# GpSimd in program order, low parts of the second layer on VectorE, and a joint form of the later heads

## The chip, the core and the metric

The kernel runs on one core of a Trainium2 chip. The metric is the time of one execution on the device in microseconds (us). The core has five engines that run side by side, each with its own instruction queue: PE (TensorE, matrix products; its weight loads are shown apart as PEld), DVE (VectorE), ACT (ScalarE), POOL (GpSimd) and SP, which only issues DMAs. An engine works through its queue in order and stands still at an instruction whose inputs are not there. POOL also issues DMAs here.

## The reference

Windowed attention, then a two-layer network on its output:

```python
scores = q @ k.T / 8                       # 8 batches, 8 heads, 576 positions, 64 wide
# heads 0-3: key within 32 positions back; heads 4-7: every 4th key within 128 back
attn = exp(masked - max); attn = attn / (attn.sum(-1) + 1e-9)
x = (attn @ v) laid out as [4608 tokens, 512]
h = x @ w_in                               # [512, 2048], float64 input
g = where(h >= 1, h, where(h <= -1, 0, (h + 1) ** 2 / 4))
out = g @ w_out                            # [2048, 512]
```

## The kernel before

**Attention.** Two heads are handled together: "head n" below is such a pair, 0 to 31, four to a batch. Queries are cut into 18 blocks of 32, and each block meets 64 keys. `scores` makes 36 small matmuls into two PSUM banks and adds the mask (L151, one DVE instruction for each of the two heads of the pair, `j`). `softmax` runs L165 to L171: the row maximum on DVE, the subtraction on POOL, the exponential on ACT, the row sum, + EPS (L169) and the reciprocal on DVE, the multiplication on POOL. The weights are then transposed, on PE for heads 0 to 11 (`transpose_pe`, L196, copied out by ACT in L204) and on DVE for heads 12 to 31 (`transpose`, L185, twelve instructions of 32x192 for each head), and `values` (L236) multiplies by v: 36 matmuls, each 64 keys deep and 32 queries wide. One matmul in this precision shows as two records in the trace.

**Network.** Numbers are kept as a high part (rounded by ACT, L284) and a low part (a subtraction, L285, on DVE or POOL), and three products of parts make one product. `split` does both. Tokens 0 to 511 go through `layer1` and `layer2` directly while the weights are turned from float64 into parts (`weights`), summed (`combine`) and written to `stream` in DRAM. The other 4096 tokens go in four passes p = 1 to 4 of 1024 tokens, where each layer is a seven-product scheme (Strassen-Winograd) on halves: `macro1` makes 56 units in the first layer, `macro2` 56 in the second; each unit is six matmuls. In the second layer unit j is product kk = j // 8 of column block u = j % 8. `make_part(p, j + 4)` prepares the operand of a unit four units ahead: for kk = 1 and kk = 2 it first combines blocks of g on DVE (L521, L523, L527), then splits. The low part goes to DVE for odd u, to POOL for even u. `ops_x` prepares the seven operands x of the next pass, four of the low parts on POOL.

**Order.** PE and SP follow the program; the order of the instructions on DVE, ACT and POOL is chosen by a scheduler from estimated costs and priorities. For passes 1 to 4 `seq` lists the units, and `place(i, fn)` hangs other work before unit i of that list: head i of a pass has its scores and softmax at base + 9i + 3, its transposes at + 9, its values at + 15. Weights are read back from `stream` by DMAs on POOL (L609), nine units ahead, into five buffers that hold two units each. In the first stage (tokens 0 to 511) `slots` does the same for heads 4 to 11.

## Time and profile before

| | us |
|---|---|
| median of 3 runs | 1048.84 (1047.24 to 1049.14) |
| the profiled execution | 1050.84 |
| its span, first to last instruction | 1049.1 |
| PE busy in the span | 904.7 (86%) |
| DVE busy | 735.1 (70%) |
| POOL busy | 554.3 (53%) |
| ACT busy | 506.9 (48%) |

The span is one execution seen by the hardware profiler; 1.7 us lie around it. Shares of busy time are means over stages that differ, so the rows further down are taken by stage: 0 to 225 us is the first stage (heads 0 to 11, the first 512 tokens, the weights), then the four passes follow, each with a first layer and a second layer. PE has two speeds; the profile gives the granted clock as a share of the full one, and in a stretch at the low level each matmul takes about twice as long.

### The profile page before, as it was taken

The page shows a single profiled execution, that of the slowest core. Times are in us where ns is not written, and L with a number is a line of the kernel's source. Part 1 is how long each engine was busy: PE and PEld are TensorE (multiplying, and loading weights), DVE is VectorE, ACT ScalarE, POOL GpSimd, SP SyncE. Part 2 cuts the span into 40 slices and gives each one's busy share as a digit, 9 for nine tenths or more (in the row PEclk, how much of TensorE's full clock was granted, in tenths as well). Part 3 has the DMA queues.
Part 4 walks back from the last instruction along what each step waited for, and adds up shares of the span by engine and source line. Part 5 has one row for each costly group of instructions (what it writes and reads, how often), then busy time and mean ns, then how long its engine had stood idle before and what let it go on. Part 6 is the DMA issues. An engine that isn't in the chain of part 4 may idle for free.

```text
span 1049.1 us, 19802 instructions
## 1 busy us (share of the span) xinstructions
PE 904.7 (86%) x7990; PEld 729.5 (70%) x7990; DVE 735.1 (70%) x1039; ACT 506.9 (48%) x779; POOL 554.3 (53%) x466
## 2 busy tenths in 40 slices
PE   4668777989988886999988797999995999999898
PEld 3656565767776664887767575887784888887686
DVE  6877888568878997447778997367869932457743
ACT  2544555444444534435535435434465443656353
POOL 2545566574434668753335465733346674324674
PEclk7578987999899888999999788999898999999899
DMA  9579983787566553786666553785453677666565
GB/s 363 206 267 347 376 286 137 267 275 231 170 188 189 165 176 115 206 245 202 192 186 191 148 165 104 237 242 154 123 163 115 172 211 229 200 192 181 145 196 161
DMA packets 104922, 212.90 MB, mean 203 GB/s; under 512 B 7872, under 2 KB 20352, under 8 KB 102784
## 3 DMA queue, kind: packets, MB, share of 16 engines
q0 software_dynamic: 60928, 117.45, 39.1%
q1 hardware_dynamic: 43904, 94.20, 25.6%
q8 instruction: 63, 1.03, 0.4%
q14 instruction: 27, 0.22, 0.1%
HBM read 172.82 MB, written 38.80 MB: 202 GB/s over the span
## 4 chain that ended last, share of the span: by engine, by line
PE 41%; DVE 32%; ACT 8%; POOL 8%; issue 7%; DMA 2%; SPq 1%; POOLq 0%; DVEq 0%; ACTq 0%
PE o_b L541 12%; PE o_c L541 8%; DVE pt L185 7%; PE h_b L470 7%; DVE g L463 4%; PE h_c L470 3%; ACT pt L459 3%; PE o_a L541 3%; DVE pt L456 3%; PE o L236 2%; POOL c L171 2%; DVE g L505 2%; PE acc L382 2%; ACT pt L462 2%; DVE m L319 2%
## 5 line engine op out<-in xcount | busy, mean ns | idle before, releaser
L470 PE MATMUL h_b<-x,wi 128*128 128x512 f32 x768 | 201.4, 407 | 23.4 <-DVE pt L456 11.5
L470 PEld LDWEIGHTS h_b<-x,wi 128*128 128x128 f32 x768 | 147.4, 195 | 60.9 <-DVE pt L456 14.1
L609 POOL DMA_DIRECT2D wi<-stream_wi x112 | 81.8, 731 | 139.8 <-PE h_b L470 62.7
L541 PE MATMUL o_b<-parts,wo 128*128 128x512 f32 x384 | 104.1, 414 | 27.0 <-DVE parts L285 19.7
L463 DVE SCALAR_TENSOR_TENSOR g<-pt 128x1536 f32<-128x1536 f32 (+1 forms) x64 | 82.0, 1302 | 57.1 <-ACT pt L462 56.5
L284 ACT CAST part<-g 128x512 fp32r<-128x512 f32 x112 | 69.3, 621 | 89.3 <-PE o_c L541 37.3
L609 POOL DMA_DIRECT2D wo<-stream_wo x112 | 82.7, 739 | 55.2 <-PE o_b L541 23.4
L541 PEld LDWEIGHTS o_b<-parts,wo 128*128 128x128 f32 x384 | 74.2, 198 | 47.1 <-DVE parts L285 22.5
L285 POOL TENSOR_TENSOR part<-g,part 128x512 fp32r<-128x512 f32 x56 | 78.6, 1404 | 53.6 <-ACT part L284 49.3
L470 PE MATMUL h_c<-x,wi 128*128 128x512 f32 x384 | 104.0, 407 | 1.7 <-DVE out L395 1.7
L185 DVE STREAM_TRANSPOSE pt<-c 32x192 f32<-32x192 f32 x240 | 88.5, 369 | 21.7 <-POOL c L171 18.6
L236 PEld LDWEIGHTS o<-pt,v 64*64 64x64 f32 x2160 | 77.0, 151 | 34.9 <-issue 12.7
L236 PE MATMUL o<-pt,v 64*64 64x32 f32 x2160 | 81.5, 233 | 22.7 <-ACT pt L204 7.7
L284 ACT CAST parts<-g 128x512 fp32r<-128x512 f32 x112 | 69.0, 620 | 61.0 <-PE o_b L541 25.4
L285 POOL TENSOR_TENSOR parts<-g,parts 128x512 fp32r<-128x512 f32 x56 | 78.6, 1404 | 37.0 <-ACT parts L284 35.9
L541 PE MATMUL o_b<-part,wo 128*128 128x512 f32 x384 | 94.1, 390 | 1.6 <-DVE part L285 1.6
L459 ACT ACTIVATE pt<-pt,consts 128x1536 f32<-128x1536 f32 x32 | 50.5, 1579 | 85.9 <-DVE pt L456 85.9
L285 DVE TENSOR_TENSOR part<-g,part 128x512 fp32r<-128x512 f32 x56 | 48.9, 874 | 60.9 <-ACT part L284 60.9
L470 PEld LDWEIGHTS h_c<-x,wi 128*128 128x128 f32 x384 | 74.5, 195 | 19.7 <-ACT out L395 2.1
L166 POOL TENSOR_TENSOR c<-c 96x768 f32<-96x768 f32 x28 | 47.2, 1687 | 76.7 <-DVE c L165 76.7
L541 PEld LDWEIGHTS o_b<-part,wo 128*128 128x128 f32 x384 | 71.8, 188 | 17.6 <-DVE part L285 2.4
L171 POOL TENSOR_TENSOR c<-c 96x768 f32<-96x768 f32 x30 | 52.8, 1759 | 51.7 <-DVE c L170 43.2
(104 smaller groups left out, 1694.9 us busy)
## 6 DMA issues: line engine op xcount, KB each, us to landing
wi<-stream_wi POOLq DMA_DIRECT2D x112, 512.0 KB, 4.3
wo<-stream_wo POOLq DMA_DIRECT2D x112, 512.0 KB, 4.1
v<-v_in SPq DMA_DIRECT2D x30, 576.0 KB, 4.3
k<-k_in SPq DMA_DIRECT2D x30, 304.0 KB, 5.0
...
```

Source lines behind the costliest of these rows:

```text
L166: eng.tensor_tensor(out=c, in0=c, in1=spread(0), op=ALU.subtract)
L171: nc.gpsimd.tensor_tensor(out=c, in0=c, in1=spread(2), op=ALU.mult)
L185: nc.vector.transpose(out=pt[r : r + 32, :, g], in_=c[32 * g : 32 * g + 32, j, :, 32 * h : 32 * h + 32],)
L236: PE.matmul(out=ops[part][r, QB * i : QB * i + QB], lhsT=hd["v"][r, at], rhs=hd["pt"][r, QB * at : QB * at + QB], start=True, stop=True,)
L284: nc.scalar.copy(out=out_hi, in_=src)
L285: lo_engine.tensor_tensor(out=out_lo, in0=src, in1=out_hi.bitcast(F32), op=ALU.subtract)
L456: nc.vector.tensor_tensor(out=o, in0=a, in1=b, op=ALU.add)
L459: nc.scalar.activation(out=src, in_=src if first_in is None else first_in, func=AF.Prelu, bias=minus_t, alpha=0.5)
L463: nc.vector.scalar_tensor_tensor(out=dst, in0=src, scalar=1.0, in1=src, op0=ALU.min, op1=ALU.mult)
L470: PE.matmul(out=bk, lhsT=w[:, a, 128 * c : 128 * c + 128], rhs=X[p, kk][:, x, c], start=STARTS[kk] and c == 0 and n == 0, stop=STOPS[kk] a ...
L541: PE.matmul(out=bk, lhsT=w[:, a, 128 * m : 128 * m + 128], rhs=s[:, x], start=STARTS[kk] and u == 0 and n == 0, stop=STOPS[kk] and u == NU ...
L609: nc.gpsimd.dma_start(out=t, in_=stream[name][i0 : i0 + 2].rearrange("c p h x -> p c h x"))
```

## The change

1. POOL follows the program order too, like PE and SP. `softmax` is cut into `exps` and `normalise`, which are placed by hand: at + 5 and + 8 of a later head, and in the slots behind the scores in the first stage.
2. In the second layer the low part goes to DVE for three of four u (kk > 0), and for one of four u at kk = 0.
3. Heads 12 to 31: one mask instruction for both heads of the pair, six transposes of 32x384 instead of twelve of 32x192 into one zeroed buffer `pts`, and values in 12 matmuls over 128 keys and 96 queries; v is loaded in a layout of its own (`v2`). Heads are 11 units apart instead of 9. The + EPS goes from DVE to ACT for all heads.
4. `stream` is 28 small tensors for each layer, and a read of two units takes one row of 4 KB for each partition, where it took two of 2 KB.
5. The steps of `ops_x` move: two POOL splits 16 and 12 units ahead of the rest, the others behind the last head's values. In the first stage the stores of weights and their preparation are put in another order.

```diff
+    pts = const.tile([128, 2, NB // 3, 96], F32, name="pts")
...
+    stream = {
+        n: [dram.tile([128, 2, 2, 256], F32, name=f"stream_{n}{i}") for i in range(7 * NU // 2)]
+        for n in ("wi", "wo")
+    }
...
+    def banks_of(which, name):
+        if which is None:
+            both = ps.tile([128, 2, TOK], F32, tag="att", name=name)
+            return both, [both[:, 0], both[:, 1]]
+        return None, [bank(i, f"{name}_{i}") for i in which]
...
+        else:
+            vt = hd["v"][:, : NB // 3 * 2 * D]
+            nc.sync.dma_start(out=vt, in_=v2[n - EARLY])
+            hd["v"] = vt.rearrange("p (j t d) -> p j t d", j=2, d=D)
...
+            else:
                 nc.vector.tensor_tensor(
-                    out=c[:, j],
-                    in0=sps[j][:96, : 6 * KW].rearrange("p (t x) -> p t x", x=KW),
-                    in1=msk[:, kind],
+                    out=c.rearrange("p j t x -> p j (t x)"),
+                    in0=both[:96, :, : 6 * KW],
+                    in1=msk[:, kind].rearrange("p t x -> p (t x)").unsqueeze(1).broadcast_to([96, 2, 6 * KW]),
                     op=ALU.add,
                 )
...
+        engine.tensor_tensor(out=c, in0=c, in1=spread(n, 0), op=ALU.subtract)
...
+    def normalise(n, engine):
+        c, st = heads[n]["c"], heads[n]["st"]
         nc.vector.tensor_reduce(out=st[:, 1], in_=c, op=ALU.add, axis=AX.X)
-        nc.vector.tensor_scalar(out=st[:, 1], in0=st[:, 1], scalar1=EPS, scalar2=None, op0=ALU.add)
+        nc.scalar.activation(out=st[:, 1], in_=st[:, 1], func=AF.Copy, bias=EPS)
         nc.vector.reciprocal(out=st[:, 2], in_=st[:, 1])
-        nc.gpsimd.tensor_tensor(out=c, in0=c, in1=spread(2), op=ALU.mult)
...
     def transpose(n):
-        c, pt = heads[n]["c"], new_pt(n).rearrange("p (t g i) -> p t g i", g=3, i=QB)
-        for j in range(2):
-            for g in range(3):
-                for h in range(2):
-                    r = 64 * j + 32 * h
-                    nc.vector.transpose(
-                        out=pt[r : r + 32, :, g],
-                        in_=c[32 * g : 32 * g + 32, j, :, 32 * h : 32 * h + 32],
-                    )
-
-    def transpose_pe(n, banks):
-        c, pt = heads[n]["c"], new_pt(n)
-        for i, (t0, t1) in enumerate(((0, 4), (4, 6))):
-            tp = bank(banks[i], f"t{n}_{i}")
+        c = heads[n]["c"].rearrange("p j t x -> p (j t) x")
+        pt = pts.rearrange("p j t i -> p (j t) i")
+        for g in range(3):
+            for h in range(2):
+                r = 32 * (g + h)
+                nc.vector.transpose(
+                    out=pt[r : r + 32, :, 32 * g : 32 * g + 32],
+                    in_=c[32 * g : 32 * g + 32, :, 32 * h : 32 * h + 32],
+                )
...
+        else:
+            for t in range(NB // 3):
                 for j in range(2):
-                    part = turn ^ j
-                    r = slice(64 * j, 64 * j + 64)
-                    at = half * part + i
                     PE.matmul(
-                        out=ops[part][r, QB * i : QB * i + QB],
-                        lhsT=hd["v"][r, at],
-                        rhs=hd["pt"][r, QB * at : QB * at + QB],
+                        out=ops[t // 3][64 * j : 64 * j + 64, 96 * (t % 3) : 96 * (t % 3) + 96],
+                        lhsT=hd["v"][:, j, t],
+                        rhs=pts[:, j, t],
                         start=True,
                         stop=True,
                     )
...
         elif kk == 2:
             nc.vector.tensor_tensor(out=g[:, B21], in0=g[:, B21], in1=g[:, B11], op=ALU.subtract)
         with tc.high_priority(offset=40):
-            split(s[:, 0], s[:, 1], g[:, source[kk]], nc.vector if u % 2 else nc.gpsimd)
+            split(s[:, 0], s[:, 1], g[:, source[kk]], nc.vector if (u % 4 if kk else u % 4 == 3) else nc.gpsimd)
...
-                nc.gpsimd.dma_start(out=t, in_=stream[name][i0 : i0 + 2].rearrange("c p h x -> p c h x"))
+                nc.gpsimd.dma_start(out=t, in_=stream[name][i0 // 2])
...
         base = index_of("l1", p, 0)
+        step = 11
         for i, n in enumerate(ns):
-            place(base + 9 * i + 3, lambda n=n: scores_step(n))
-            place(base + 9 * i + 9, lambda n=n: transpose(n))
-            place(base + 9 * i + 15, lambda n=n: values_step(n))
-        for i, fn in enumerate(ops_x(p + 1)):
-            place(base + 9 * len(ns) + 10 + i, fn)
+            at = base + step * i
+            place(at + 2, lambda n=n: scores_step(n))
+            place(at + 5, lambda n=n: exps(n, nc.gpsimd))
+            place(at + 8, lambda n=n: normalise(n, nc.gpsimd))
+            place(at + 11, lambda n=n: transpose(n))
+            place(at + 16, lambda n=n: values_step(n))
+        steps = ops_x(p + 1)
+        free = index_of("l1", p, 7 * NU - 1) + 2
+        end = max(base + step * (len(ns) - 1) + 16, free + 10)
+        for i, fn in enumerate(steps):
+            place(max(end - 16, free) + 4 * i if i < 2 else end + i - 1, fn)
...
-        slot(s0 + 4, lambda n=n: transpose_pe(n, ATT))
+            slot(s0 + 1, lambda n=n: exps(n, nc.gpsimd))
+            slot(s0 + 2, lambda n=n: normalise(n, nc.gpsimd))
+        slot(s0 + 4, lambda n=n: transpose_pe(n))
         slot(s0 + 6, lambda n=n: values_step(n))
-        if n == 9:
-            slot(s0 + 7, lambda: ops_first[0]())
     ops_first = ops_x(1)
-
-    with tc.manual_schedule(engines={mybir.EngineType.PE, mybir.EngineType.SP}):
+    slot(29, ops_first[0])
+    slot(30, ops_first[1])
...
+    with tc.manual_schedule(
+        engines={mybir.EngineType.PE, mybir.EngineType.SP, mybir.EngineType.Pool}
+    ):
         for n in range(4):
-            scores(n, (2 * n, 2 * n + 1))
-            softmax(n, fast=n < 2)
+            scores(n, (2 * n, 2 * n + 1) if n < 3 else None)
+            if n > 1:
+                exps(n - 2, nc.vector)
+        exps(2, nc.gpsimd)
+        normalise(0, nc.gpsimd)
+        exps(3, nc.gpsimd)
+        normalise(1, nc.gpsimd)
         load_qk(4)
...
+        transpose_pe(0, (0, 1))
+        normalise(2, nc.gpsimd)
+        values(0, (2, 3))
+        normalise(3, nc.gpsimd)
         weights("wi", 0)
-        transpose_pe(0, (0, 1))
-        values(0, (2, 3))
         transpose_pe(1, (4, 5))
-        values(1, (6, 7))
+        values(1)
...
-            if s % 2 == 0 and s < NF:
-                u = s // 2
-                keep_base("wi", u)
-                keep_sums("wi", u)
+            u = s // 2
+            if s % 2 == 0:
+                if u < NU:
+                    keep_base("wi", u)
+                    keep_sums("wi", u)
+                    if u:
+                        combine("wo", u)
+                if 0 < u <= NU:
+                    keep_sums("wo", u - 1)
+                if u + 1 < NU:
+                    combine("wi", u + 1)
+            elif u < NU:
+                keep_base("wo", u)
                 if u + 2 < NU:
                     weights("wi", u + 2)
-                if u + 1 < NU:
-                    combine("wi", u + 1)
-                if 2 * u + 9 < len(order):
-                    fetch(2 * u + 9)
-            elif s < NF:
-                u = s // 2
-                keep_base("wo", u)
-                keep_sums("wo", u)
-                if u + 2 < NU:
-                    weights("wo", u + 2)
-                if u + 1 < NU:
-                    combine("wo", u + 1)
-                if 2 * u + 10 < len(order):
-                    fetch(2 * u + 10)
+                for i in (2 * u + 9, 2 * u + 10):
+                    if i < len(order):
+                        fetch(i)
             if 2 <= s < NF:
                 layer2(s - 2)
+            if s % 2 and 2 <= s and u + 1 < NU:
+                weights("wo", u + 1)
             for fn in slots.pop(2 * s + 1, ()):
                 fn()
...
+        assert not slots, slots.keys()
+        prefetch(2 * DEPTH - 1)
         layer2(NF - 2, range(2))
-        for fn in ops_first[1:]:
+        nc.gpsimd.memset(pts, 0.0)
+        for fn in ops_first[2:]:
             fn()
```

The first place is POOL in the second layer of pass 1, where the operands of pass 2 (x) are split. `part` and `parts` are low parts of the units, x_5 and x_0 splits of 128x1024, wo the reads of weights. Before, from unit 16 on:

```order
L285 TENSOR_TENSOR part_16_3918<-g_0_2558,part_16_3918 128x512
L609 DMA wo_22_3947<-stream_wo 128x2x512
L285 TENSOR_TENSOR parts_3679<-g_2_2895,parts_3679 128x512
L609 DMA wo_24_3971<-stream_wo 128x2x512
L285 TENSOR_TENSOR part_20_3979<-g_4_3151,part_20_3979 128x512
L609 DMA wo_26_3997<-stream_wo 128x2x512
L285 TENSOR_TENSOR parts_3679<-g_6_3497,parts_3679 128x512
L609 DMA wo_28_4063<-stream_wo 128x2x512
L285 TENSOR_TENSOR x_5_4202<-raw,x_5_4202 128x1024
L285 TENSOR_TENSOR part_24_4071<-g_0_2558,part_24_4071 128x512
L609 DMA wo_30_4083<-stream_wo 128x2x512
```

Now, from the same part on:

```order
L322 TENSOR_TENSOR part_16_3610<-g_0_2554,part_16_3610 128x512
L647 DMA wo_22_3626<-stream_wo_110 128x1024
L197 TENSOR_TENSOR c_3508<-c_3508 96x768
L647 DMA wo_24_3654<-stream_wo_111 128x1024
L322 TENSOR_TENSOR part_20_3662<-g_4_3041,part_20_3662 128x512
L322 TENSOR_TENSOR x_0_3686<-raw,x_0_3686 128x1024
L647 DMA wo_26_3689<-stream_wo_112 128x1024
L647 DMA wo_28_3754<-stream_wo_113 128x1024
L322 TENSOR_TENSOR part_24_3762<-g_0_2554,part_24_3762 128x512
L322 TENSOR_TENSOR x_1_3774<-raw,x_1_3774 128x1024
L647 DMA wo_30_3777<-stream_wo_114 128x1024
```

Between part_16 and part_24 POOL had three other low parts and the split x_5; now it has one low part (part_20), the multiplication of a head (L197) and the split x_0, and x_1 follows part_24.

The second place is DVE in the first layer of pass 1, around the softmax of one head (c). Names: pt and g are the activation of the first layer, c the weights of a head. Before:

```order
L456 TENSOR_TENSOR pt_1_2517<-h_1_b,pt_1_2517 128x512
L456 TENSOR_TENSOR pt_2_2651<-h_2_a,pt_2_2651 128x512
L185 STREAM_TRANSPOSE pt_2726<-c_2572 32x6x32 x12
L456 TENSOR_TENSOR pt_1_2517<-h_1_c,pt_1_2517 128x512
L463 SCALAR_TENSOR_TENSOR g_1_2721<-pt_1_2517 128x512
L151 TENSOR_TENSOR c_2766<-s_6_2767,msk 96x384
L151 TENSOR_TENSOR c_2766<-s_7_2768,msk 96x384
L165 TENSOR_REDUCE c_2766<-c_2766 96x12
L463 SCALAR_TENSOR_TENSOR g_1_2721<-pt_1_2517 128x1536
```

Now, around the same head:

```order
L194 TENSOR_REDUCE c_2584<-c_2584 96x12
L494 TENSOR_TENSOR pt_1_2522<-h_1_c,pt_1_2522 128x512
L196 RECIPROCAL c_2584<-c_2584 96x12
L211 STREAM_TRANSPOSE pts<-c_2584 32x12x32 x6
L501 SCALAR_TENSOR_TENSOR g_1_2692<-pt_1_2522 128x1536
L501 SCALAR_TENSOR_TENSOR g_1_2692<-pt_1_2522 128x512
L494 TENSOR_TENSOR pt_2_2644<-h_2_b,pt_2_2644 128x512
L543 TENSOR_TENSOR g_1_2692<-g_1_2692 128x512
L494 TENSOR_TENSOR pt_3_2737<-h_3_a,pt_3_2737 128x512
L176 TENSOR_TENSOR c_2762<-s_2763,msk 96x768
L188 TENSOR_REDUCE c_2762<-c_2762 96x12
```

The twelve transposes of 32x6x32 have become six of 32x12x32, the two masks of 96x384 one of 96x768, and the + EPS between L168 and L170 is gone from DVE, so that the reciprocal (L196) stands behind an ACT instruction.

The third place is POOL in the first stage, around the softmax of head 6 (c). w_ and sum_ are weights and sums of weights. Before:

```order
L285 TENSOR_TENSOR sum_wi_1_873<-m_706,sum_wi_1_873 128x2x256
L166 TENSOR_TENSOR c_974<-c_974 96x768
L285 TENSOR_TENSOR w_wo_800<-m_706,w_wo_800 128x1024
L171 TENSOR_TENSOR c_974<-c_974 96x768
L285 TENSOR_TENSOR sum_wo_0_1043<-m_706,sum_wo_0_1043 128x2x256
L285 TENSOR_TENSOR sum_wo_1_1046<-m_706,sum_wo_1_1046 128x2x256
```

Now:

```order
L322 TENSOR_TENSOR w_wi_1050<-m_1046,w_wi_1050 128x1024
L322 TENSOR_TENSOR w_wo_1072<-m_823,w_wo_1072 128x1024
L189 TENSOR_TENSOR c_1000<-c_1000 96x768
L197 TENSOR_TENSOR c_1000<-c_1000 96x768
L322 TENSOR_TENSOR sum_wo_0_1155<-m_823,sum_wo_0_1155 128x2x256
L322 TENSOR_TENSOR sum_wo_1_1158<-m_823,sum_wo_1_1158 128x2x256
```

The subtraction and the multiplication of the head, with one low part between them before, now stand one right behind the other.

## Rows read from the trace of the kernel before

**Rows 1.** The page, part 1: busy time, share, instructions.

```profile
PE 904.7 (86%) x7990; PEld 729.5 (70%) x7990; DVE 735.1 (70%) x1039; ACT 506.9 (48%) x779; POOL 554.3 (53%) x466
```

**Rows 2.** Windows by stage: length, busy times with counts, granted clock, DMA share, GB/s.

```profile
0.00:225.00 225.00, 168.45 (x2405) 138.33 (x2406) 165.61 (x221) 110.18 (x186) 124.44 (x78) 0.82 0.79 282
225.00:341.00 116.00, 101.26 (x1131) 80.15 (x1130) 93.53 (x151) 55.59 (x82) 52.25 (x45) 0.97 0.65 200
341.00:404.00 63.00, 52.87 (x524) 41.95 (x522) 60.58 (x93) 30.03 (x51) 38.36 (x31) 0.89 0.56 173
404.00:455.00 51.00, 41.46 (x171) 33.71 (x171) 22.90 (x25) 23.37 (x38) 42.79 (x34) 0.90 0.59 171
455.00:565.00 110.00, 100.63 (x1133) 80.45 (x1132) 79.57 (x141) 53.15 (x77) 44.83 (x43) 0.97 0.66 197
565.00:633.00 68.00, 54.31 (x520) 43.66 (x519) 64.10 (x93) 28.65 (x49) 37.01 (x31) 0.85 0.55 161
633.00:682.00 49.00, 44.63 (x178) 36.11 (x178) 24.71 (x26) 22.92 (x38) 34.50 (x33) 0.90 0.62 182
682.00:784.00 102.00, 97.61 (x912) 78.56 (x911) 69.67 (x118) 49.99 (x71) 39.05 (x38) 0.93 0.58 169
784.00:815.00 31.00, 18.88 (x68) 14.40 (x67) 29.50 (x25) 17.72 (x24) 17.97 (x14) 0.82 0.41 118
956.00:977.00 21.00, 15.36 (x63) 11.62 (x62) 19.62 (x21) 10.81 (x16) 10.72 (x10) 0.95 0.49 148
```

**Rows 3.** Waits, whole span: total us, times, longest.

```profile
POOL c L171 <- DVE c L170: 43.2, 17, 4.6
POOL wi L609 <- PE h_b L470: 62.7, 31, 4.5
PE o_b L541 <- DVE parts L285: 19.7, 5, 6.5
PE o_c L541 <- POOL part L285: 9.1, 1, 9.1
```

**Rows 4.** Timeline of PE: start, us, instruction and count.

```profile
191.35 1.21 PE L196 MATMUL t<-ident,c 96*64 96x96 f32 x24
...
376.32 2.29 PE L236 MATMUL o<-pt,v 64*64 64x32 f32 x72
```

**Rows 5.** Groups by line, shapes apart: busy us, mean ns, idle before.

```profile
L185 DVE STREAM_TRANSPOSE pt<-c 32x192 f32<-32x192 f32 x240 | 88.5, 369 | 21.7 <-POOL c L171 18.6
L609 POOL DMA_DIRECT2D wo<-stream_wo x112 | 82.7, 739 | 55.2 <-PE o_b L541 23.4 <-PE h_c L470 18.0 <-PE h_b L470 7.6
L285 POOL TENSOR_TENSOR part<-g,part 128x512 fp32r<-128x512 f32 x56 | 78.6, 1404 | 53.6 <-ACT part L284 49.3 <-issue 4.2
L285 DVE TENSOR_TENSOR part<-g,part 128x512 fp32r<-128x512 f32 x56 | 48.9, 874 | 60.9 <-ACT part L284 60.9
L151 DVE TENSOR_TENSOR c<-s,msk 96x384 f32<-96x384 f32 x60 | 30.4, 545 | 8.3 <-PE s L141 8.1
L168 DVE TENSOR_REDUCE c<-c 96x12 f32<-96x768 f32 x30 | 28.3, 944 | 17.4 <-ACT c L167 17.3
L169 DVE TENSOR_SCALAR c<-c 96x12 f32<-96x12 f32 x30 | 6.6, 221 | 0.6
```

**Rows 6.** Timeline of DVE, pass 1, the same line at two times.

```profile
332.51 4.33 DVE L505 TENSOR_TENSOR g<-g 128x512 f32<-128x512 f32 x1
...
369.20 0.68 DVE L505 TENSOR_TENSOR g<-g 128x512 f32<-128x512 f32 x1
```

**Rows 7.** Timeline of POOL, pass 1, second layer, splits of x.

```profile
399.33 12.61 POOL L285 TENSOR_TENSOR x<-raw,x 128x1024 fp32r<-128x1024 f32 x1
...
415.86 2.41 POOL L285 TENSOR_TENSOR x<-raw,x 128x1024 fp32r<-128x1024 f32 x1
```

**Rows 8.** DMA issues: KB each, median us from issue to landing.

```profile
wi<-stream_wi POOLq DMA_DIRECT2D x112, 512.0 KB, 4.3
```

93 lines of the change are left out of this document (59 added, 34 removed).

## The prediction, made before the changed kernel ran

> **What bounds the kernel now.** The first thing to read is the page's line of busy times [rows 1]: PE is busy for 904.7 of 1049.1 us, so 144 us of the span are PE standing still, and no other engine is near its limit on the mean. The second view is the windows by stage [rows 2], since the mean hides the limit of each stage. The length of a window less PE's busy time gives PE's standstill: 56.5 us in the first stage; 14.7, 9.4 and 4.4 in the first layers of passes 1 to 3 (225 to 341, 455 to 565, 682 to 784); 10.1, 13.7, 12.1 and 5.6 where the second layer of a pass starts (341 to 404, 565 to 633, 784 to 815, 956 to 977); 9.5 and 4.4 in the middle of the second layer of passes 1 and 2 (404 to 455, 633 to 682). What matters is DVE in the same rows: 93.5 of 116 us, then 60.6 of 63, 64.1 of 68, 29.5 of 31. Where PE stands still, DVE is full; in the middle of the second layer it is at half (22.9 of 51), and there POOL is full (42.8 of 51).
>
> The granted clock in these rows is the second loss. A window at 0.85 is one in which PE spent part of the time at 1.2 instead of 2.4 GHz, and the low values stand in the windows with the waits. PE's busy time times what is missing to 1 gives 39.5 us over the nine windows after 225, and 30 in the first stage.
>
> The third view, the waits [rows 3], names the late partner: PE at the second layer waits for low parts from DVE (19.7 us in 5 waits) and once 9.1 us for a low part from POOL. POOL in turn waits for DVE's reciprocal (43.2) and, with its DMAs, for PE to free a buffer (62.7), so it runs in step with PE and not ahead.
>
> The last view is the timelines at these spots. The same DVE instruction takes 4.33 us at 332.5 and 0.68 at 369.2 [rows 6]; a split of x on POOL takes 12.61 us at 399.3 and 2.41 at 415.9 [rows 7]. The long one on POOL is the 9.1 us wait of PE: the low part stood behind it. Both kinds read two operands from SBUF, and neither waits for an input in that time. So DVE and POOL block each other, and the cost of an instruction on one is paid on the other. The Trainium skill says the same (SBUF — State Buffer, Who interferes with whom: a VectorE instruction with two SBUF inputs contends with a GpSimd instruction that reads SBUF, and the later one blocks fully); the traces agree, but 12.61 us is longer than any one instruction, so the loser can lose several times in a row.
>
> **The change part by part.** I sum against the profiled execution (1050.84 us; its span 1049.1 plus 1.7) and go to the median of the runs, 2.0 lower, at the end.
>
> *Values of the 20 later heads, on PE.* Now 72 records in 2.29 us [rows 4]. The new form has 12 matmuls, 24 records, of 96 columns. The trace has no such instruction with 128 keys, but the transposes on PE of the first stage are 24 records of 96 columns with 64 weight columns, alternating between the same two column halves, 96 keys deep: 1.21 us [rows 4]. Bounds: nothing gained to 1.08 us for each head, 0 to -21.6; a loss has no reason, since fewer records move the same columns. I take -17: the row that it is nearest to, and some of it in stretches where PE waits for DVE anyway. The Trainium skill (TensorE: Matmul & The Clock Gate, Part 3: Packing small matmuls) says that a weight load overlaps running matmuls only if the row group differs. It speaks against the new form, which uses all rows each time, while the old one alternates between halves. By it the gain would be near 0; the transposes also use the same rows each time and still take 1.21, so the sum goes by the row.
>
> *DVE in the first layer.* For each later head DVE had 2 masks of 545 ns, 2 reductions of 944, + EPS 221 and 12 transposes of 369 [rows 5], 7.63 us with the reciprocal left out. Now: one mask over 768 columns, 0.94 like the reduction over 768; two reductions; six transposes of double length. From masks and reductions (384 to 768 columns: +399 ns) 192 columns more cost 0.2, so 0.57 for each; bounds 0.37 and 0.74, for the head 2.2 to 4.4 us. Together 6.24. With 11 units between heads instead of 9, 5.1 heads instead of 6.2 fall on 56 units: 47.3 us become 31.8, and DVE in the 225 to 341 window goes from 93.5 to about 78. Of PE's 28.5 us of waits in first layers, 6.3 belong to the handover from the first stage and stay. I take half of the other 22, -11; bounds 0 and -22.
>
> *Start of the second layer.* Here two effects meet. At kk = 0 six of eight low parts are POOL's and the heads no longer end there; at kk = 1 and 2 DVE has two more low parts each, and later heads reach into it. DVE's list from the fifth head's mask to the end of kk = 2 has the same number of two-operand instructions to within one or two, less the shorter transposes. So the stretch gets easier by a little. Of 41.5 us I take a third, -14; bounds 0 and -30.
>
> *The splits of x.* Before, POOL had three low parts and x_5 between part_16 and part_24; now one low part, a multiplication and x_0, and x_1 has another four units. Nothing but a low part of four units later stands behind it, so a split that is held up for 8 us (six units at 1.45, from 171 matmuls in 41.46 us [rows 2]) costs PE nothing. Of 13.9 us of waits (9.5 and 4.4) I take -9; bounds 0 and -13.9.
>
> *The clock.* These three are 34 of 84 us of waits after 225. With them go low stretches; of 39.5 us I take 12, since many waits remain and each can bring one.
>
> *Low parts from POOL to DVE,* 10 for each pass, 40 in all: 1.40 us each on POOL, 0.87 on DVE [rows 5]. In the second layer from kk = 3 PE is the bound, so nothing is gained at once; the cover is that DVE has room. Its load there: 24 low parts of 0.87, one and a half heads of 6.24 and seven instructions on 1024 columns at twice 0.68: 40 of 46 us. That is close. + EPS on ACT adds a wait: the reciprocal stands behind ACT's queue, and what stands behind it on DVE (transposes, sums of products) waits too. I put +5 on both; bounds 0 and +40.
>
> *First stage.* POOL has the same instructions, in program order. Subtraction and multiplication of a head often stand directly behind each other, so POOL stands still while DVE and ACT do the sums: up to 4.6 us each time [rows 3]; in return the head's weights are ready earlier, and PE's waits are mostly for these. POOL is busy for 124.4 of 225, DVE for 165.6 [rows 2]; DVE loses 12 x 0.22 and some mask time. I take -3; bounds -32 and +20.
>
> *Rows of 4 KB, v of late heads, order of stores:* 0. A read lands 4.3 us after its issue [rows 8] and is asked for nine units, 13 us, ahead; no PE wait in the trace is for it. POOL's issue is 739 ns [rows 5]; if half of that went, POOL would still wait for PE. If the cover went, each late read would cost what is over 13 us.
>
> Sum: -17 - 11 - 14 - 9 - 12 + 5 - 3 = -61, 1050.8 - 61 = 989.8, as a median 988.
>
> **The rivals.**
> (a) *The first stage gains as well.* For it: PE's waits there are the largest item, 56.5 us and 30 of clock, and heads late in the softmax are their cause. Against: DVE's work is not less. If 40% of the waits and 30% of the clock went, -32 instead of -3: 959.
> (b) *Values as dear as before and the start of the second layer as full.* For it: the rule on weight loads above, and DVE at 60.6 of 63 us with nearly the same list. Against: the 1.21 us. Terms 1 and 3 are 0 and half of the clock's stays: -61 + 17 + 14 + 6 = -24, as a median 1025.
> (c) *Slower: low parts on DVE wait for POOL in the second layer.* Place: units 24 to 55 of each pass. A low part on DVE that finds POOL at a low part waits up to 1.40 us, DVE is at 40 of 46 us, and PE has only four units of lead. If one in three of the 24 waits that long, 11 us in each pass, and about 9 reach PE: +37 in four passes; x splits and layer starts then gain nothing either, +35. -61 + 72 = +11: 1060. It decides from about one in four on. Against: DVE's mean over such low parts is 0.87 today, with POOL doing half of them, and there will be fewer POOL ones.
> (d) *The waits only move*: within 2 us of before.
>
> **How the numbers follow.** Forecast 56%, (a) 15%, (b) 17%, (c) 9%, (d) 3%. The likeliest alone spans 965 to 1010. The range for 8 in 10 reaches from just under (a), since its bound is open, to over (b): 957 to 1035. Faster by over 0.2%, which is about what a measurement of this kernel tells from no change: 56 + 15 + 17 = 88%; within it 3%; slower 9%.
>
> **What would show it.** The values of late heads: about 1.2 us for 24 records; at 2.2, (b). DVE between two heads of a first layer: gaps instead of 93 of 116 us, transposes at 0.57. Splits of x on POOL may still be long, but without a PE wait on a low part behind them. Second layers from kk = 3: PE without gaps; gaps "o_b or o_c behind DVE parts" there mean (c). First stage: its length against 225 us decides between forecast and (a). What would make me wrong most: a first stage much shorter or longer than I say, since I have no term for it but an order.

## The result and the profile after

The changed kernel takes 1019.39 us (median of 4 runs, 1017.94 to 1024.86), before 1048.27; the ratio is 0.9734 [0.9696, 0.9772]. Forecast was 988, so the direction is right and less than half of the gain came. A second measurement gave 1020.39, ratio 0.9739 [0.9715, 0.9763]. The windows by stage of the kernel after, cut so that each row holds the work of a row of [rows 2] (the first stage now ends at 256.4, before at 224.8; both hold 2404 or 2405 PE records):

```profile
core 0: us, PE busy (x) PEld busy (x) DVE busy (x) ACT busy (x) POOL busy (x), PEclk, DMA share, GB/s
...
0.00:256.00 256.00, 177.85 (x2404) 144.47 (x2404) 164.49 (x204) 116.29 (x201) 131.26 (x83) 0.78 0.71 250
256.00:349.00 93.00, 90.40 (x793) 72.13 (x794) 75.40 (x94) 52.50 (x81) 36.71 (x40) 0.98 0.69 217
349.00:412.00 63.00, 49.43 (x452) 37.02 (x451) 58.24 (x72) 28.05 (x52) 36.37 (x30) 0.95 0.53 169
412.00:460.00 48.00, 44.25 (x200) 34.24 (x200) 40.78 (x45) 25.69 (x44) 27.53 (x26) 0.96 0.63 201
460.00:550.00 90.00, 87.71 (x792) 70.05 (x791) 66.50 (x89) 50.90 (x77) 32.77 (x39) 1.00 0.69 216
550.00:613.00 63.00, 49.47 (x452) 36.98 (x451) 58.24 (x72) 28.04 (x51) 36.58 (x30) 0.95 0.54 168
613.00:661.00 48.00, 44.28 (x200) 34.21 (x199) 40.96 (x45) 25.69 (x44) 27.40 (x26) 0.96 0.63 202
661.00:752.00 91.00, 87.81 (x724) 69.85 (x723) 64.33 (x84) 49.61 (x75) 30.47 (x38) 1.00 0.62 191
752.00:780.00 28.00, 17.08 (x66) 12.54 (x65) 24.53 (x19) 14.70 (x20) 14.74 (x12) 0.93 0.36 112
780.00:927.00 147.00, 142.79 (x605) 115.97 (x604) 84.72 (x105) 74.15 (x106) 56.49 (x66) 0.97 0.64 193
927.00:949.00 22.00, 17.81 (x69) 13.61 (x68) 18.28 (x17) 14.17 (x20) 10.08 (x10) 0.92 0.43 137
```

Two things stand in it. The passes, 824.3 us before (224.8 to 1049.1), take 762.0 (256.4 to 1018.4): -62, and the forecast's terms for them add up to -58. The first stage is 31.6 us longer (31 by the rounded windows), where the forecast had -3. Of this 6.0 us are the wait for the first streamed weights, which now stands ahead of the first unit of pass 1; before, the waits of this handover (6.3 us) stood behind it and counted to the passes. Counted alike, the first stage is 25.6 us longer and the passes are 56 shorter. In the first layers PE now hardly waits (93.0 less 90.4, 90.0 less 87.7, 91.0 less 87.8); where the second layers start it waits as before (13.6, 13.5, 10.9).

What PE waits for in the first stage, and below it what POOL waits for there, first after the change and then before it:

```profile
PE t L222 <- POOL c L197: 20.3, 5, 7.4
PE t L222 <- ACT pts L230: 14.2, 8, 5.7
PE h L390 <- DVE x L244: 8.9, 1, 8.9
...
PE h_b L508 <- DMA wi<-stream_wi: 6.0, 1, 6.0
```

```profile
POOL sum_wo L322 <- ACT sum_wo L321: 32.9, 8, 8.1
POOL c L197 <- DVE c L196: 19.0, 5, 5.7
```

```profile
PE t L196 <- POOL c L171: 9.4, 3, 7.8
PE h L353 <- DVE x L218: 4.3, 3, 2.8
POOL c L171 <- DVE c L170: 17.6, 6, 4.6
POOL sum_wo L285 <- ACT sum_wo L284: 5.0, 2, 4.1
```

The second and the fourth of the PE waits were absent before. The two longest, 8.9 and 7.4 us, are of one kind. The timelines around the 8.9, of DVE, POOL and PE:

```profile
57.99 7.91 DVE L340 TENSOR_SCALAR raw_wo<-raw_wo 128x1024 uint32<-128x1024 uint32 x1 [1.37 <-DMA raw_wo<-w_in]
65.82 1.13 DVE L244 TENSOR_TENSOR x<-o,x 128x256 fp32r<-128x256 f32 x2
...
83.16 0.69 DVE L340 TENSOR_SCALAR raw_wo<-raw_wo 128x1024 uint32<-128x1024 uint32 x1
```

```profile
46.47 2.40 POOL L322 TENSOR_TENSOR w_wi<-m,w_wi 128x1024 fp32r<-128x1024 f32 x1 [11.39 <-ACT w_wi L321]
52.80 1.47 POOL L189 TENSOR_TENSOR c<-c 96x768 f32<-96x768 f32 x1 [3.92 <-DVE c L188]
56.70 1.47 POOL L197 TENSOR_TENSOR c<-c 96x768 f32<-96x768 f32 x1 [2.44 <-DVE c L196]
58.13 2.48 POOL L322 TENSOR_TENSOR sum_wi<-m,sum_wi 128x512 fp32r<-128x512 f32 x2
60.57 2.33 POOL L322 TENSOR_TENSOR w_wo<-m,w_wo 128x1024 fp32r<-128x1024 f32 x1
62.87 2.48 POOL L322 TENSOR_TENSOR sum_wo<-m,sum_wo 128x512 fp32r<-128x512 f32 x2
65.31 1.72 POOL L322 TENSOR_TENSOR sum_wi<-m,sum_wi 128x512 fp32r<-128x512 f32 x1
```

```profile
67.01 3.35 PE L390 MATMUL h<-x,w_wi 128*128 128x512 f32 x7 [8.91 <-DVE x L244]
```

DVE's shift takes 7.91 us beside a series of POOL splits without a gap, and 0.69 at 83.16. PE's next operand stood behind it. At 127.0 it is the same: a DVE instruction of 7.22 us (1.22 where nothing is beside it) beside the subtraction and two splits on POOL, then the sum of a head, its multiplication, and PE after 7.36 us. POOL does the steps in the order of the program. Ahead of the series it stood 11.4 us for ACT's part of w_wi and 6.4 us for a head's row maximum and reciprocal on DVE, with the six splits behind that; ACT had finished its part of all six by 51.4 us. The hold at 58 us is in all five profiles with POOL in program order in the first stage (7.2 to 8.3 us; the changed kernel twice, e1, e15 and e4), while in the three where POOL is scheduled there (e2, e3, e5) no DVE instruction of that stage takes more than 4.1 us. The one at 127 us is missing in the second profile of the changed kernel, whose first stage is only 1.6 us shorter. The shift at 58 us has one operand in SBUF; the Trainium skill (SBUF — State Buffer, Who interferes with whom) says that a tensor_scalar can also enter the mode that contends with GpSimd. The trace agrees, 7.91 against 0.69.

The forecast instructions are there (groups by line: busy time, mean ns): values at 1.21 us for each of the 20 heads against 2.29, transposes at 568 ns against 570 forecast, reads of the first layer's weights at 546 against 731, of the second's at 557 against 739.

```profile
L273 PE MATMUL o<-pts,v 128*64 128x96 f32 x480 | 24.2, 250 | 6.9 <-DVE c L176 6.9
...
L211 DVE STREAM_TRANSPOSE pts<-c 32x384 f32<-32x384 f32 x120 | 68.2, 568 | 17.3 <-POOL c L197 15.8
...
L647 POOL DMA_DIRECT2D wi<-stream_wi x112 | 61.1, 546 | 182.9 <-PE h_b L508 91.4 <-PE h_c L508 42.3 <-PE h_a L508 24.4
```

### The profile page after: what moved, and what is told of

Its sections match the earlier page's. It is cut to its first block, busy times and chain, and to the rows that moved or that the text cites. A ratio compares the mean times of both kernels' runs of the same rounds, so it can differ in the third digit from the quotient of the medians.

```text
span 1018.4 us, 17699 instructions
## 1 busy us (share of the span) xinstructions
PE 874.4 (86%) x7030; PEld 694.8 (68%) x7030; DVE 737.2 (72%) x898; ACT 510.7 (50%) x811; POOL 467.6 (46%) x427
## 4 chain that ended last, share of the span: by engine, by line
PE 36%; DVE 29%; ACT 11%; issue 9%; POOL 9%; DMA 4%; SPq 2%; POOLq 0%; ACTq 0%; DVEq 0%
PE o_b L579 10%; PE o_c L579 7%; PE h_b L508 6%; DVE g L501 5%; ACT pt L497 4%; DVE pts L211 3%; DVE parts L322 3%; PE h_c L508 3%; ACT pt L500 3%; DVE pt L494 2%; PE o_a L579 2%; PE h L390 2%; POOL c L189 2%; DVE m L343 2%; PE h_a L508 2%
## 5 line engine op out<-in xcount | busy, mean ns | idle before, releaser
L508 PE MATMUL h_b<-x,wi 128*128 128x512 f32 x768 | 193.5, 399 | 11.3 <-DMA wi<-stream_wi 6.0
L647 POOL DMA_DIRECT2D wi<-stream_wi x112 | 61.1, 546 | 182.9 <-PE h_b L508 91.4
L322 POOL TENSOR_TENSOR part<-g,part 128x512 fp32r<-128x512 f32 x64 | 97.5, 1524 | 72.4 <-ACT part L321 72.1
L579 PE MATMUL o_b<-parts,wo 128*128 128x512 f32 x384 | 102.1, 408 | 33.4 <-DVE parts L322 17.1
L501 DVE SCALAR_TENSOR_TENSOR g<-pt 128x1536 f32<-128x1536 f32 x64 | 90.6, 1443 | 54.8 <-ACT pt L500 54.6
L322 DVE TENSOR_TENSOR parts<-g,parts 128x512 fp32r<-128x512 f32 x104 | 101.8, 991 | 16.9 <-ACT parts L321 13.7
L647 POOL DMA_DIRECT2D wo<-stream_wo x112 | 62.3, 557 | 75.0 <-PE o_b L579 28.2
L497 ACT ACTIVATE pt<-pt,consts 128x1536 f32<-128x1536 f32 x32 | 50.5, 1577 | 65.8 <-DVE pt L494 65.8
L211 DVE STREAM_TRANSPOSE pts<-c 32x384 f32<-32x384 f32 x120 | 68.2, 568 | 17.3 <-POOL c L197 15.8
L500 ACT ACTIVATE pt<-pt,consts 128x1536 f32<-128x1536 f32 x64 | 73.6, 1155 | 0.2
L197 POOL TENSOR_TENSOR c<-c 96x768 f32<-96x768 f32 x30 | 49.6, 1655 | 49.8 <-DVE c L196 49.7
L189 POOL TENSOR_TENSOR c<-c 96x768 f32<-96x768 f32 x28 | 52.9, 1889 | 39.7 <-DVE c L188 39.6
L390 PE MATMUL h<-x,w_wi 128*128 128x512 f32 x192 | 60.7, 474 | 10.0 <-DVE x L244 8.9
L322 DVE TENSOR_TENSOR part<-g,part 128x512 fp32r<-128x512 f32 x48 | 41.2, 858 | 32.5 <-ACT part L321 32.1
```

What stands on the lines that cost most here:

```text
L189: engine.tensor_tensor(out=c, in0=c, in1=spread(n, 0), op=ALU.subtract)
L197: engine.tensor_tensor(out=c, in0=c, in1=spread(n, 2), op=ALU.mult)
L211: nc.vector.transpose(out=pt[r : r + 32, :, 32 * g : 32 * g + 32], in_=c[32 * g : 32 * g + 32, :, 32 * h : 32 * h + 32],)
L322: lo_engine.tensor_tensor(out=out_lo, in0=src, in1=out_hi.bitcast(F32), op=ALU.subtract)
L390: PE.matmul(out=hp, lhsT=w[:, a, f % 2, 128 * c : 128 * c + 128], rhs=X[0, c // 2][:, x, c % 2], start=c == 0 and n == 0, stop=c == NC - 1 ...
L497: nc.scalar.activation(out=src, in_=src if first_in is None else first_in, func=AF.Prelu, bias=minus_t, alpha=0.5)
```

## Experiments on the first stage

Theory A: the transposes on PE wait falsely on the joint tile (both halves of a head's transposes now lie in one PSUM tile over two banks, and the second half waits until ACT has copied the first). Theory B: POOL's program order. Theory C: the new order of weights and stores. Below, "start" is the time at which PE begins the first unit of pass 1, 256.4 us in the changed kernel.

**Transposes whole (e1, e15).** The 12 matmuls of both halves stand ahead of ACT's copies:

```diff
         for tp, (t0, t1) in zip(tps, ((0, 4), (4, 6))):
             ... matmuls
-            with tc.high_priority(offset=60):
-                nc.scalar.copy(...)
+        for tp, (t0, t1) in zip(tps, ((0, 4), (4, 6))):
+            with tc.high_priority(offset=60):
+                nc.scalar.copy(...)
```

> The changed kernel, but the transposes on PE of heads 0 to 11 are emitted as one run of 12 matmuls, with ACT's two copies behind them, so that the second half no longer waits for ACT's copy of the first half (14.2 us of PE waits in the first stage of the changed kernel's profile; before there were none). Theory A (the joint PSUM tile makes a false wait, and this is what lengthened the first stage): the passes start about 15 us earlier than 256.4, near 241, and the kernel takes 1002 to 1008. Theory B (POOL in program order brings the heads' weights late): PE only comes earlier to the next wait for POOL or DVE; the passes start at 250 or later, the kernel 1013 or more. Theory C (the new order of weights, sums and stores): as B.

> The kernel of the first experiment once more (transposes emitted whole, all else as changed), for a second profile of it. If the give-back is a matter of how DVE and POOL happen to meet in a second layer, its second layers of passes 1 and 2 are again 91 to 99 us, and not the same ones as the first time; the passes start at 244 to 246 and the time lies between 1012 and 1025. If the earlier start itself costs the passes 10 us: both second layers at 98 again.

Measured 1024.5 (1018.4 to 1025.5) and 1025.85 (1022.6 to 1029.1): not faster. The waits behind the copies are gone, the passes start at 244.7 and 251.7, but PE waits 33.4 us (7 times) for POOL's multiplication instead of 20.3 (5 times), and each second layer of passes 1 and 2 takes 97 to 99 us, not 93. So A alone isn't the loss. e15's expectation of 244 to 246 was wrong, and both second layers long again is what it had given as a sign that the early start itself costs; the table below speaks against that.

**POOL left to the scheduler in the first stage (e2); there with the old order too (e3); both edits (e5).**

```diff
-    with tc.manual_schedule(engines={PE, SP, Pool}):      # first stage
+    with tc.manual_schedule(engines={PE, SP}):
...
+    with tc.manual_schedule(engines={PE, SP, Pool}):      # from the memset of pts on
```

> The changed kernel, but in the first stage POOL's order is left to the scheduler again; from the first pass on it follows the program. Theory B: the waits of PE for POOL's multiplication (20.3 us in 5) fall to about the 9.4 of before, the passes start about 15 us earlier, near 241, the kernel takes about 1004. Theory A: the 14.2 us behind ACT's copies stay, the passes start at 250 or later, kernel 1013 or more. Theory C: no change, 1017 to 1021.

> As the run before this one (POOL left to the scheduler in the first stage), and the weights, sums, stores and fetches of the first stage are put back in the order of the kernel before. To be compared with that run. Theory C (the new order costs): the passes start at least 10 us earlier than in that run. Theories A and B: within 4 us of it. If this run starts its passes near 225, order and POOL together are the whole loss and the joint tile costs nothing.

> The changed kernel with both edits at once: transposes on PE emitted whole, and POOL in the first stage left to the scheduler. If the false wait on the joint tile and POOL's program order are the whole excess of the first stage (256.4 against 224.8), and independent, the passes start at 256.4 - 11.6 - 22.7 = 222. If the second edit already contains the first, they start at 232 or later. The kernel then takes 992 to 1000 in the first case, as the passes gain 62 as in the changed kernel; 1003 to 1006 in the second, or in the first if what is won in the first stage is given back in the second layers.

e2: 1005.42, ratio 0.9588 [0.9572, 0.9604], start at 233.7: 22.7 earlier; the waits for POOL's multiplication fall to 5.4 and the 8.9 to 3.3:

```profile
PE t L222 <- POOL c L197: 5.4, 1, 5.4
PE h L390 <- DVE x L244: 3.3, 1, 3.3
```

The wait of 6.0 for the first weights is gone from ahead of the start too; 3.5 us of waits stand behind it instead.

e3: 1022.42 (0.9752 [0.9723, 0.9781]), start at 236.4, 2.7 behind e2: the order of weights and stores costs nothing in the first stage; C falls. e5: 992.88, ratio 0.9471 [0.9445, 0.9497], start at 221.4, which is 12.3 ahead of e2. B and A together are the whole loss: 256.4 - 22.7 - 12.3 = 221.4, 3.4 ahead of the kernel before. Each start is from one profile; the kernels further down that keep e5's two edits start at 222.3 to 225.9, so the 12.3 of A may be nearer 10.

**Reads ahead of the splits of x (e4).**

```diff
                     if u:
                         combine("wo", u)
+                    if u == NU - 1:
+                        prefetch(6)
```

> The changed kernel, but the first three reads of streamed weights are issued on POOL ahead of the two splits of x at the end of the first stage, instead of behind them. Only the handover changes: the wait of 6.0 us of the first unit for its weights goes. Expected: the passes start 4 to 6 us earlier, the kernel takes 1013 to 1016. If the store of the sums that the buffer holds is late instead, POOL stands there and nothing is gained, 1018 to 1021.

The start is 6.4 us earlier (250.0), about as expected, the time is not: 1025.64 (1020.4 to 1030.1). In its profile the first layer of pass 1, from its first unit to its last, takes 116 us instead of 111 and one second layer 97.

**Why an earlier start was given back.** PE, SP and POOL follow the program, but DVE's order is the scheduler's, and an edit in the first stage changes it in the passes. Two orders occur in the second layers of passes 1 and 2; they are the same list with 22 lines of difference (e3 and e4 part from order 2 in pass 2 by 2 and 4 lines more). The place where they first part, in pass 2, in the changed kernel (-) and in e2 (+); `c25` is head 25, `g2_7` the g of unit 7 of pass 2:

```diff
 L543 TENSOR_TENSOR g2_7<-g2_7 128x512
+L196 RECIPROCAL c25<-c25 96x12
 L559 TENSOR_TENSOR g2_6<-g2_6 128x512
 L501 SCALAR_TENSOR_TENSOR g2_7<-pt2_7 128x512
-L196 RECIPROCAL c25<-c25 96x12
 L322 TENSOR_TENSOR parts2<-g2_7,parts2 128x512
-L559 TENSOR_TENSOR g2_7<-g2_7 128x512
 L211 STREAM_TRANSPOSE pts<-c25 32x12x32
```

| kernel | start of passes | second layer, pass 1 | pass 2 |
|---|---|---|---|
| changed | 256.4 | 93, order 1 | 93, order 1 |
| e1 | 244.7 | 97, order 2 | 98, order 2 |
| e15 | 251.7 | 99, order 2 | 98, order 2 |
| e2 | 233.7 | 91, order 1 | 97, order 2 |
| e3 | 236.4 | 99, order 2 | 101, order 2 |
| e4 | 250.0 | 91, order 1 | 97, order 2 |
| e5 | 221.4 | 91, order 1 | 92, order 1 |

(From the end of the last unit of the first layer to the next pass's first one, in us.) Order 1 takes 91 to 93 without exception, order 2 97 to 101. An early start alone doesn't cost this: e2 and e5 start earliest and have 91 in pass 1. In e2's profile 11 of the 22.7 us are given back: 5.3 in pass 2, the one with order 2, and 2.0, 2.3 and 1.4 in the other passes. So order 2 is the largest single part of what e2 gives back, not all of it. No run set DVE's order by hand, so that the order is the cause is argued from this table and not tested by itself. e16 repeats the changed kernel:

> The changed kernel once more, for a second profile. If DVE's order decides over a second layer (one order in all passes measured at 91 to 93 us, the other at 97 to 99), its second layers of passes 1 and 2 are 91 to 94 again, since its program has the first order in both. If they are 97 or more, the two orders are not the cause. The start of the passes: 250 to 257, if the first stage varies by the 7 us by which that of the kernel with whole transposes did.

Start at 254.8, second layers 91 and 92, both in order 1. Where the orders differ, other instructions of DVE are held. In e1, two of DVE's sums that take 1.21 us in the changed kernel stand beside four POOL instructions:

```profile
383.44 6.23 DVE L566 TENSOR_TENSOR g<-g 128x512 f32<-128x512 f32 x2
```

```profile
383.50 1.49 POOL L197 TENSOR_TENSOR c<-c 96x768 f32<-96x768 f32 x1
384.93 0.59 POOL L648 DMA_DIRECT2D wo<-stream_wo  x1
385.54 1.28 POOL L323 TENSOR_TENSOR part<-g,part 128x512 fp32r<-128x512 f32 x1
386.77 2.34 POOL L323 TENSOR_TENSOR x<-raw,x 128x1024 fp32r<-128x1024 f32 x1
```

But the changed kernel has a hold of 4.90 us at the same point, on the low part behind these sums (shown in step 4 below), so this place alone isn't the 5 us. Over the whole second layer of pass 1 DVE is busy for 83.2 us in the changed kernel and for 87.5 in e1, with 99 instructions in each:

```profile
367.00:459.60 92.60, 80.57 (x517) 61.37 (x516) 83.17 (x99) 43.70 (x79) 55.94 (x48) 0.96 0.59 185
355.40:452.70 97.30, 81.06 (x518) 62.21 (x517) 87.54 (x99) 43.50 (x79) 53.46 (x48) 0.95 0.55 176
```

## Experiments on the passes

**The joint form alone (e6)**, added to the kernel before: `pts`, `v2`, `transpose` and the late branch of `values` from the diff, memset of `pts` ahead of pass 1; masks and everything else as before.

```diff
+                        lhsT=hd["v"][:, j, t],
+                        rhs=pts[:, j, t],
```

> The kernel before, with only the joint form of heads 12 to 31 added: six transposes of 32x384 into one zeroed buffer and values in 12 matmuls over 128 keys; masks, + EPS, order, steps and POOL's scheduling as before. By the forecast's terms: values -17; DVE has 12 x 369 - 6 x 568 = 1.0 us less for each head, some 6 us in each of three first layers, worth -3 to -8 in all; some clock: 1019 to 1027. If the values stood in PE's idle time anyway: 1035 to 1043. The first stage stays at 225.

1004.91, ratio 0.9586 [0.9566, 0.9606]: -43, not -21 to -29. PE's busy time after 224 us falls from 736.2 to 700.6, of which 28.5 stand in the values (55.1 to 26.6) and 7 in the rest of PE's work, whose records are the same to within two, so that is the clock (granted 0.94, now 0.96). What is left of the 43 is waits. This one part gives more than the whole change.

**Who makes the low parts (e7, e9, e10), and x (e13, e14).** Theory D: DVE and POOL block each other, so DVE gets time back for each low part that POOL no longer makes. Theory E: DVE's list is what is too long. On e5, `make_part` is edited; e13 also leaves POOL to the scheduler in the passes, and e14 adds x:

```diff
-nc.vector if (u % 4 if kk else u % 4 == 3) else nc.gpsimd
+nc.vector if u % 2 else nc.gpsimd                                          # e7
+nc.vector if (kk in (1, 2) or u % 4 if kk else u % 4 == 3) else nc.gpsimd   # e9
+nc.vector if (kk or u % 4 == 3) else nc.gpsimd                             # e10, e13, e14
...
-            sp(0, b11, nc.gpsimd),      # and sp 1, 5, 6
+            sp(0, b11, nc.vector),      # e14
```

> As the run with both edits, but the low part goes to DVE for odd u only and to POOL for even u, as before the change. By the forecast's term (low parts on DVE cost 5) it is 3 to 7 us faster than that run. By the forecast's rival (low parts on DVE stand behind POOL in the second layer) 10 us or more faster. If POOL, which now waits in program order, becomes the late one for the low parts: slower by 5 to 20.

> As the run with both edits, but for kk = 1 and 2 all low parts go to DVE (16 of 16 instead of 12; POOL keeps its quarter from kk = 3). It asks why the start of the second layer, 62 to 64 us in passes 1 and 2, did not get shorter. Theory D (DVE and POOL block each other there: a low part on POOL holds up DVE's two-operand instructions for as long as DVE saves by it): DVE's busy time in the stretch stays at 57 to 59 us or falls although it has four more instructions, the stretch is 58 to 64 us and the kernel 985 to 995. Theory E (the length of DVE's list): DVE has 4 x 0.68 = 2.7 us more in each pass and PE waits for it: 65 to 67 us, the kernel 6 to 12 us slower than the run with both edits.

> As the run before this one, and from kk = 3 on all low parts go to DVE too (24 more instructions than there in four passes... six for each pass). DVE is at 41 of 47 us in the middle of the second layer of passes 1 and 2 with both edits. Theory D: POOL then has only the splits of x and the heads there, DVE's mean for a low part falls from 0.94 to under 0.80, and PE waits no more than before: 985 to 996. Theory E: 6 x 0.68 = 4 us more bring DVE to 45 of 47, low parts come late, and it is 5 to 20 us slower than the run with both edits.

> Transposes emitted whole, POOL left to the scheduler everywhere, and all low parts from kk = 1 on given to DVE: the edits that won together. The two last won 9.4 and 8.6 us over the run with both edits. Theory D (DVE and POOL block each other; with nearly no low part on POOL, POOL's order hardly matters): they overlap, 978 to 983. If they were independent: 975. Theory E (DVE's list): 984 or more.

> As the run before this one, but the four low parts of x that POOL makes for each pass are DVE's too (128x1024, 2.41 us on POOL, 1.21 on DVE when neither is held up). Theory D: POOL holds DVE up no more near the end of the second layer, 2 to 8 us faster than the run before this one. Theory E: 4 x 1.21 us more on DVE in a stretch where it is at 39 of 44 us, PE waits for low parts: 5 to 15 us slower.

e7 1006.5 (ratio 0.9594 [0.9568, 0.9619]), e5 992.88, e9 993.39, e10 984.24 (0.9394 [0.9367, 0.9420]), e13 984.25, e14 964.89 (0.9214 [0.9198, 0.9229]). Each step towards DVE holds or wins; theory E fell in e10 and e14, e9 alone decides little (stretches of 66 and 63 us). In e10 the mean of DVE's low parts falls from 0.94 to 0.80 us, as theory D had it. (Over e9 it moves 32 low parts, eight for each pass, not six.) e13 came out 1 us over what theory D gave, just inside theory E's range: its two edits win the same thing. e14 won 19, more than expected. The lines of busy times of e7, e5, e10, e13 and e14, in this order, say why:

```profile
PE 870.0 (87%) x7030; PEld 693.7 (69%) x7030; DVE 731.6 (73%) x858; ACT 511.7 (51%) x811; POOL 515.8 (51%) x467
```

```profile
PE 867.1 (88%) x7030; PEld 690.5 (70%) x7030; DVE 736.5 (75%) x898; ACT 511.5 (52%) x811; POOL 469.7 (48%) x427
```

```profile
PE 862.6 (88%) x7030; PEld 689.7 (70%) x7030; DVE 741.5 (75%) x946; ACT 510.5 (52%) x811; POOL 402.9 (41%) x379
```

```profile
PE 863.3 (88%) x7030; PEld 688.7 (70%) x7030; DVE 718.3 (73%) x946; ACT 509.7 (52%) x811; POOL 400.6 (41%) x379
```

```profile
PE 865.5 (89%) x7030; PEld 691.1 (71%) x7030; DVE 722.5 (75%) x962; ACT 510.9 (53%) x811; POOL 362.3 (37%) x363
```

From e7 to e10 DVE takes over 88 instructions, 60 us at 0.68 each, and is busy for 10 us more; from e13 to e14 16 more of 1.21, 19 us, and it is busy for 4 us more. In the start of the second layer of pass 2 it is 68 instructions in 60.43 us (e7) and 80 in 59.95 (e10):

```profile
526.00:590.00 64.00, 50.32 (x452) 38.90 (x451) 60.43 (x68) 28.60 (x51) 36.81 (x30) 0.89 0.51 165
```

```profile
522.00:586.60 64.60, 52.57 (x452) 40.31 (x451) 59.95 (x80) 27.91 (x51) 29.67 (x26) 0.87 0.53 172
```

These edits also change the order of DVE's other instructions. In passes 1 to 3, low parts and x left out, e9 and e10 have the same order to within one line; so the 9 us from e9 to e10 are the move's, with 32 instructions (22 us at 0.68) for 8.3 us of DVE's busy time. From e7 to e5 20 lines differ in each of these passes, from e13 to e14 32, 22 and 6; how much of those 14 and 19 us is the order's isn't shown.

**POOL free in the passes (e11), step 9 (e12), x split with the others (e8).**

```diff
-    with tc.manual_schedule(engines={PE, SP, Pool}):      # e11: {PE, SP} everywhere
-        step = 11                                         # e12: 9
-            place(max(end - 16, free) + 4 * i if i < 2 else end + i - 1, fn)
+            place(end + i - 1, fn)                        # e8
```

> As the run with both edits, but POOL is left to the scheduler in the passes as well. If the program order on POOL is what keeps the splits of x from standing ahead of a low part (the 9.1 us wait of the kernel before), such a wait comes back and the kernel is 3 to 15 us slower, 996 to 1008. If the gain of the passes has nothing to do with POOL's order: 988 to 997.

> As the run with both edits, but the heads of a pass are 9 units apart as before, not 11: one more head falls in the first layer and one less in the second. The forecast took the wider step as a part of DVE's relief in the first layers (47 to 32 us of head work, together with the shorter instructions; with step 9, 39). By that the first layers are 2 to 4 us longer each, and the second layers shorter by as much or more, since there DVE is the fuller one: 985 to 995. If first layers are again held up by DVE: 996 to 1004.

> As the run with both edits, but the two splits of x on POOL that the change puts 16 and 12 units ahead stand with the other steps behind the last head. In the changed kernel's second layers one split of x on POOL lies beside DVE's sums and low parts and DVE is held for 4 to 6 us there. If that hold is what decides between second layers of 93 and of 98 us, they are 91 to 93 here and the kernel 3 to 10 us faster than the run with both edits. If the splits now meet the other ones at the end, PE waits for a low part there, and it is as before, or up to 9 us in a pass slower.

e11 983.49 (0.9379 [0.9348, 0.9411]): program order costs 9 us in the passes too, against both expectations. With POOL nearly empty it doesn't matter (e10 and e13 are equal). Nor do the last low parts matter once POOL is scheduled (e11 and e13 are equal): in these runs the move wins only beside a POOL in program order. e12 1007.06, beyond both expectations: the wider step is worth 14 us. e8 994.84, equal to e5: the early split of x decides nothing in the time, and its second layers (94 and 96 us, in a third order) are not the 91 to 93 that were expected.

**How far it goes.** On e14, in e17 the softmax of later heads on DVE (`exps(n, nc.vector)`, `normalise(n, nc.vector)`), in e18 half of the low parts of kk = 0 (`kk or u % 2`).

> As the run with x on DVE, but the subtraction and the multiplication of the softmax of heads 12 to 31 go to DVE too, so that POOL only issues DMAs and makes three low parts in four of kk = 0 in the passes. DVE gets 2 x 0.94 us for each head, 38 in all, about 9 us in a first layer where it is at 67 of 90. Blocking alone (theory D): POOL's 1.5 to 4.3 us for each go, the chain of a head is shorter, 950 to 963. Length of DVE's list (theory E): the start of the second layer, at 54 of 60 us, has two heads more to do, 970 to 985.

> As the run with x on DVE, but of the low parts of kk = 0 DVE makes every second instead of every fourth: two more for each pass, at the end of the first layer where DVE also makes the g of the last units. Theory D: 0 to 5 us faster, 960 to 965. Theory E: PE waits longer for the low parts of kk = 0, 966 to 972.

965.58 and 966.81, as e14: nothing more is won. The first lies between the ranges of the two theories, the second in theory E's, so theory D's forecast of a further gain failed in both. The best version is e14, 54 us under the changed kernel.

## Why the prediction was wrong, by its own steps

1. **First stage, -3 (bounds -32 and +20): +31. This step failed,** at the place that the prediction itself called its weakest. It set POOL's waits for one head's sums (4.6 us) against earlier weights; these waits hardly changed (17.6 us in 6, now 19.0 in 5). It missed that the splits of weights, which wait for ACT, stand in the same order, pile up behind whatever POOL waits for, and then run in series that block DVE; 22.7 us by e2. The length of POOL's waits for ACT isn't what costs: in e2 they are as long (20.7 us for sum_wi and 19.8 for sum_wo; in the changed kernel 1.5 and 32.9). What differs is what stands behind them. It had no term at all for the joint PSUM tile, which makes the second half of the transposes wait for the copy of the first; 12.3 us from e2 to e5. Of the 31, 22 are waits (56.5 to 78.2, of them 6.0 the handover) and 9 are PE's busy time at a granted clock of 0.78 instead of 0.82. With both removed, e5 is at 992.9, near the forecast; in part by luck, since terms 4 and 7 below were wrong and others made up for them.
2. **Values, -17:** 2.29 to 1.21 us for each head, -21.6, the edge of its bounds. Seven of the 20 heads had taken longer than 2.29 before (2.6 to 4.9, five of them at a granted clock of 0.50 to 0.79), so the busy time of the values fell by 30.9:

```profile
225.00:1049.10 824.10, 55.07 (x1440) 51.70 (x1440) 0.00 (x0) 19.52 (x70) 0.94 0.61 181
256.40:1018.40 762.00, 24.22 (x480) 20.45 (x480) 0.00 (x0) 19.65 (x70) 0.97 0.61 190
```

The half of rival (b) by the rule on weight loads is out. Its other half, a start of the second layer as full as before, came true (step 4); that its 1025 lies near 1019 is chance, since the loss is in the first stage.

3. **DVE in the first layers, -11:** waits other than the handover 22.2 to 8.1, -14.
4. **Start of the second layer, -14: not there,** 41.5 to 42.2. Counting DVE's instructions was the error: DVE is at 58.2 of 63 us with 72 instead of 93 [rows 2], and part of this is standing inside them. Of the 13.6 us in pass 1 the largest two waits are 4.5 for a low part from POOL and 4.1 for one from DVE, which took 4.90 us (0.68 where it isn't held) beside a low part and the split of x that the change put there:

```profile
362.89 1.97 PE L579 MATMUL o_b<-parts,wo 128*128 128x512 f32 x4 [4.49 <-POOL parts L322]
...
395.13 4.90 DVE L322 TENSOR_TENSOR parts<-g,parts 128x512 fp32r<-128x512 f32 x1
395.91 1.27 POOL L322 TENSOR_TENSOR part<-g,part 128x512 fp32r<-128x512 f32 x1
397.14 2.34 POOL L322 TENSOR_TENSOR x<-raw,x 128x1024 fp32r<-128x1024 f32 x1
400.09 1.68 PE L579 MATMUL o_b<-parts,wo 128*128 128x512 f32 x4 [4.07 <-DVE parts L322]
```

5. **Splits of x, -9:** 13.9 to 7.5, -6.4. The 9.1 us wait behind POOL is gone, waits of 3 to 4 us behind DVE came.
6. **Clock, -12:** PE's busy time in the passes fell by 39.6. With 21.6 of it for the values that is -18, half of which lies in the slow heads of step 2; the rest of PE's work fell by 8.7.
7. **Low parts to DVE and + EPS, +5: wrong sign for the first.** e7 puts the low parts back and loses 13.6, a change of DVE's order included. That lies in the range which its expectation gave for a late POOL, but it is DVE's low parts that PE waits for more (o_b behind DVE's parts 30.5 us in 9 waits against 14.4 in 6 in e5, behind POOL's 9.7 against 12.6). The argument (DVE at 40 of 46 us) left out what DVE gets back when POOL stops. In the places of rival (c) PE waits 4.2 us from 780 to 927 (before 0 of 141), but 7.5 instead of 13.9 in passes 1 and 2 (step 5); the rival had 37 more over four passes. + EPS was not tried alone.

The passes: -21.6 - 18 - 22.7 of waits (88 to 65, the handover now in the first stage) = -62. Steps 4 and 7 failed there and 2, 3 and 6 made up for it.

Not settled: how the 22.7 us divide between DVE blocked by POOL and PE waiting for a late multiplication, which hang together; how much of e7's, e5's and e14's distances is DVE's order; and why the changed kernel's runs spread over 7 us.
